# One level of Strassen's scheme for the two channel products of batches 2 to 7, on blocks of 288 positions

## The chip, the cores and the metric

The kernel runs on one core of one Trainium2 chip. The metric is the device time of one execution in microseconds; before the change it was 920.71 us (median of 3 runs, 919.43 to 924.66). The core's engines are called PE (matrix products), DVE, ACT and POOL (elementwise work, reductions, copies) and SP (which here only issues transfers). Each works its own instructions in program order, and they wait for one another by semaphores.

## What is computed

For each of 8 batches (8 heads, 576 positions, head size 64): a pooled attention (q, k, v averaged over 4 positions, the result repeated 4 times) plus a local attention (only positions less than 4 apart), then a mixer over 576 positions and 512 channels.

```
x = pooled_attention(q, k, v) + local_attention(q, k, v)    # [8, 576, 512]
h = max(x^T @ w_tok1, 0) @ w_tok2                           # 576 -> 256 -> 576, over positions
u = x + h^T
out = u + max(u @ w_ch1, 0) @ w_ch2                         # 512 -> 1536 -> 512, over channels
```

The last line holds the two channel products that the change is about.

## The kernel before, in words

Every value of a channel product is split into two f16 parts, hi and lo, and a product is three matmuls: hi x hi, hi x lo, lo x hi (`PASSES`, `mm3`, L116 to L118). Both weights, split and scaled, stay in SBUF for the whole run (`C1.fin`, `C2.fin`; tile names CW and CX). Channels lie on the partitions, positions along the free dimension, and a batch's 576 positions are worked as two chunks of 256 and 320 (`CHUNKS`).

For a chunk, `first` (L746) makes 12 blocks of 128 hidden channels, each of 4 x 3 matmuls into one of the three banks "m"; `first_up` (L760) takes each bank out twice: ACT writes relu as hi (L765), DVE the rest as lo (L767). `second` (L770) makes 4 blocks of 128 output channels, each of 12 x 3 matmuls; `second_up` (L784) has DVE scale the bank and add it to u (L793), and SP stores it (L794). So a batch has 2 x (12 x 12 + 4 x 36) = 576 matmuls of these.

Beside the products of batch b goes side work for the next batches, emitted in the same program order by a pacing rule: after each block `tick` (L898) takes as many side steps as a budget allows (`SIDE`, L888; a step counts by its written PE time). `side` (L735) is attention of batch b+1 in the order of the list `ORDER`, and then, by turns, its mixing (`mix`, L581) and the loads and poolings of batch b+2 (`ahead`, L723).

- `pooled` (L452), four times a batch: PE scores sd, DVE maximum and difference (pd), ACT exponential, PE transposes (td), ACT copy (ptd), PE product (ad), DVE normalization (rd, od; L494 to L496). The last one stores od into the rows of vw by transfers on ACT's queue (L502).
- `local` (L507), five tiles of 128 positions (the last 64): PE scores (sc), DVE mask, maximum, difference, ACT exponential, DVE sum and normalization (tile P), PE transposes (pT) and product with vw (av), ACT copies (pt, x).
- `mix`: x split for the position products (xh), two position products in banks t, u taken out of the banks (L661), its maximum over the whole chunk (L663, `everywhere` L565), and its split into the f16 parts uh (L680 ACT, L682 DVE).
- `load_v` (L401): POOL adds neighbouring rows of v (L425, L426). `load`, `load_w`: transfers of qk and vw on SP's queue.

PSUM has 8 banks: two pairs "gg", three "m", one "g". In batches 1 and later "g" serves the banks ad and pT of the attention and the small ones of `everywhere`.

Batch 0 and the preparation of the weights are ordered by a planner with costs and due times (`drive`, L157); from batch 1 on the loop at L890 writes the order.

Of the kernel before, what the change touches and what calls it, by code (L numbers as in the profile page):

```python
# [22 lines left out]
CHUNKS = ((0, 256), (256, 320))  # L23
TILES = ((0, 128), (128, 128), (256, 128), (384, 128), (512, 64))
OF_CHUNK = ((0, 1), (2, 3, 4))
NMAX = 320
PASSES = ((0, 0), (0, 1), (1, 0))
FR = 0.9
LIVE = 3
# [5 lines left out]
l0+l4 l0 l4 l2 l2 l4 l4 l1+l2 l1 l2 l3 l3 l4 l4 l3+l4 l3 l4"""  # L35
# [3 lines left out]
def tile_ups_attention_mixer(ctx, tc, qk, vw, vr, w1, w2, c1, c2, out):  # L39
# [12 lines left out]
    sb = ctx.enter_context(tc.tile_pool(name="sb", bufs=1))  # L52
    psum = ctx.enter_context(tc.tile_pool(name="psum", bufs=1, space=bass.MemoryType.PSUM))
    BUFS = dict(cw=6, h=5, w=4, xh=3, x=5, u0=4, u1=8, uh0=4, uh1=4, qk=4, qd=1, vw=2, vd=1, pt=2, od=1, sm=12, ev=8, sc=24)

    SLOTS = dict(gg=2, m=3, g=1, w=4)
# [9 lines left out]
    def T(shape, dt, tag, name):  # L66
        if tag == "w":
            return sb.tile(shape, dt, tag=slot(tag), name=name, bufs=1)
        return sb.tile(shape, dt, tag=tag, name=name, bufs=BUFS[tag])

# [16 lines left out]
    junk = sb.tile([128, 512], BF16, name="junk")  # L87
# [22 lines left out]
    PT = [sb.tile([128, H, 64], F32, name=f"P{i}") for i in range(3)]  # L110
# [4 lines left out]

    def mm3(ps, lhs, rhs, first, last, **kw):  # L116
        for i, (a, c) in enumerate(PASSES):
            nc.tensor.matmul(ps, lhs(a), rhs(c), start=first and i == 0, stop=last and i == 2, **kw)  # L118
# [111 lines left out]
    def token_weight(i, n, f):  # L230
        yield step("A", 0.0, ("W", "raw", i))
        raw = made["W", "raw"][i]
        if i < len(TILES):
            y = WY[i] = T([f.shape[0], n], F32, "u1", f"W1_y{i}")
# [18 lines left out]
    def singles(n, name):  # L253
        return [sb.tile([128, 512], F32, name=f"{name}{i}") for i in range(n)]
# [70 lines left out]
    class Second(Channel):  # L325
# [26 lines left out]
        def loads(self):  # L352

            self.raws = made["C2", "raw"] = []
            for i in range(NF):
# [3 lines left out]
                else:  # L359
                    if i % 2 == 0:  # L360
                        yield step("S", 0.1, *(("av", 0, t) for t in range(len(TILES))), *([("C2", "read", i - 4), ("C2", "read", i - 3)] if i >= 8 else []))
                        two = T([128, 2, 1024], U32, "vw", f"C2_raws{i}")
                    t = two[:, i % 2]
# [5 lines left out]
    C1.place = singles(NF + 2, "CW")  # L369
# [3 lines left out]
    short = TILES[-1][1]  # L373
    x_last = [sb.tile([128, 4, 2, D], F32, name=f"x_last{i}") for i in range(2)]
    for t in (W1[-1].bitcast(F32), *x_last):
        nc.gpsimd.memset(t[short:], 0.0)
    W2 = [sb.tile([128, 2, S], F32R, name=f"W2_{k}") for k in range(2)]
    W2_y = sb.tile([128, 2, S], F32, name="W2_y")
    WY = {len(TILES) + 2 * k + j: W2_y[:, k, HS * j:HS * j + HS] for k in range(2) for j in range(2)}
    W1_PIECES = [(u32(w1[s0:s0 + n]), 256) for s0, n in TILES]  # L380
# [20 lines left out]
    def load_v(st):  # L401
# [4 lines left out]
        def fetch(i):  # L406
            pr, g = divmod(i, 2)

            tag = "w" if st.b > 1 else "x" if st.b or i < BUFS["x"] else "xh"
# [4 lines left out]
        early = {0: 8, 1: 5}.get(st.b, 0)  # L414
# [15 lines left out]
    def load_w(st):  # L430
        st.vw = []
        for h in range(2):
            t = T([128, HG, 256], F32, "vw", f"vw{st.b}_{h}")
            for par in range(2):
                nc.sync.dma_start(t[64 * par:64 * par + 1 + WB].rearrange("p g c -> p (g c)"), vw[st.b, h, par])
            st.vw.append(t)
# [15 lines left out]
    def pooled(st, pr):  # L452
# [37 lines left out]
        if pr == 0:  # L490
            st.od = T([G, 2, 2, 4, D], F32, "od", f"od{b}")
        r = T([G, 2, 2], F32, "sm", f"rd{b}_{pr}")
# [3 lines left out]
        nc.vector.tensor_tensor(st.od[:, :, :, pr], ps[:, :, :, :D], r.unsqueeze(3).to_broadcast([G, 2, 2, D]),  # L496
                                ALU.mult)
        if pr == 3:
            yield step("A", 0.2, ("vw", b), at=e)
            for h in range(2):  # L500
                for par in range(2):
                    nc.scalar.dma_start(st.vw[h][64 * par + 1 + WB:64 * par + KB],  # L502
                                      st.od[:, h, par].rearrange("p a d -> p (a d)"))
# [3 lines left out]
    def local(st, t):  # L507

        b = st.b
        s0, n = TILES[t]  # L510
        nb = n // QB
# [3 lines left out]
        for hp in range(4):  # L515
            for j in range(nb):
                g = s0 // QB + j
# [5 lines left out]
        pp = PT[(len(TILES) * b + t) % 3]  # L523
# [27 lines left out]
        for hp in range(4):  # L551
            for j in range(nb):
                h, g = divmod(s0 // QB + j, HG)
                for par in range(2):
                    p = slice(64 * par, 64 * par + KB)
                    nc.tensor.matmul(ps[QB * j:QB * j + QB, par, D * hp:D * hp + D], pt[p, hp, QB * j:QB * j + QB],  # L556
                                     st.vw[h][p, g, D * hp:D * hp + D], start=True, stop=True)
        make(("av", b, t), e)
        e = yield step("A", 0.59, give="gg")
        x = st.x[t] = x_last[b % 2] if n == short else T([n, 4, 2, D], F32, "x", f"x{b}_{t}")  # L560
# [20 lines left out]
    def mix(st):  # L581
# [3 lines left out]
        st.hid, st.acc, banks, umx = [], [], {}, []  # L585
# [14 lines left out]
        def products():  # L600
            for t in range(NT):
# [4 lines left out]
                for f in range(2):  # L606
                    if b == 0:
                        n = TILES[t][1]
# [6 lines left out]
            for ch in range(2):  # L615
                s0, N = CHUNKS[ch]
                for c in range(4):
                    e = yield step("P", 1.2, *(("W", "split" if b else "y", NT + i) for i in range(4)), ("hid", b),
                                   *([("over", b - 1, 0)] if b and ch == 0 else []), take="" if c % 2 else f"gg>{b}")
                    if c % 2 == 0:  # L620
                        banks[ch, c // 2] = P2(f"t2_{b}_{ch}_{c}")
                    whole = banks[ch, c // 2][:, c % 2]
                    ps = whole[:, :N]
                    for i, t in enumerate(OF_CHUNK[ch]):
                        o = TILES[t][0] - s0
# [344 lines left out]
```

## Time and profile before

| | |
|---|---|
| Median of 3 runs | 920.71 us (919.43 to 924.66) |
| Profiled execution: time; span of the profile | 923.04 us; 921.2 us |
| Granted PE clock, mean | 0.992 |
| Product matmuls (L118, c) | 2 x 2304, 304.5 and 304.8 us busy |
| Product matmuls of batches 2, 3, 4, 5, 6, 7 begin at | 300.0, 409.9, 519.1, 628.6, 737.7, about 847 us |
| Transfers | 68.29 MB, mean 74 GB/s |

How to read it. Times are microseconds from the span's start unless marked ns. A group's line names the line of the code, the engine, the operation, output<-input, shapes and count; then its busy time, the mean of one in ns, and the engine's idle time just before with what ended it. Busy times by stretch give for each engine the time in which it had at least one instruction under way. Instructions may overlap their neighbours, so means times counts can exceed the time that a row of them takes. A chain piece is a stretch of the chain of work that ended last. The product matmuls of batch 0 begin at 82.4 us.

### The profile page before, as it was taken

How to read it: one execution, taken by the hardware profiler on the slowest of the kernel's cores; microseconds unless marked ns; L12 is line 12 of the kernel's file. 1: busy time of each engine (PE TensorE's matmuls, PEld its weight loads, DVE VectorE, ACT ScalarE, POOL GpSimd, SP SyncE). 2: the span in 40 equal slices, each digit the busy share in tenths (PEclk: the TensorE clock that was granted, in tenths of full speed). 3: DMA queues.
4: the chain of work that ended last, by engine and by line, in shares of the span. 5: the costliest groups of instructions: out<-in, count | busy, mean ns of one | idle time of the engine just before them, and what ended most of it. 6: DMA issues, size and time to landing. Idle time of an engine off the chain costs nothing.

```text
span 921.2 us, 25682 instructions
## 1 busy us (share of the span) xinstructions
PE 886.2 (96%) x11371; PEld 703.8 (76%) x11376; DVE 477.8 (52%) x1167; ACT 294.6 (32%) x622; POOL 108.3 (12%) x191
## 2 busy tenths in 40 slices
PE   8598999999999998999999999999999999999998
PEld 4466788889777886778867797787877788777876
DVE  8678895665532755247542565327553275324221
ACT  3368454232321414124131332314232141422120
POOL 7351400121200030000300003000130000000000
PEclk9799999999999999999999999999999999999999
DMA  8894503411700035000520006200170000000000
GB/s 238 232 314 159 160 9 94 138 49 38 219 2 23 9 106 151 9 22 3 183 73 8 23 14 198 47 15 17 37 213 8 23 9 26 14 8 22 13 12 29
DMA packets 28222, 68.29 MB, mean 74 GB/s; under 512 B 3504, under 2 KB 14000, under 8 KB 26864
## 3 DMA queue, kind: packets, MB, share of 16 engines
q1 hardware_dynamic: 25552, 64.30, 23.5%
q10 hardware_dynamic: 2560, 2.36, 0.9%
q8 instruction: 89, 1.46, 0.7%
q14 instruction: 21, 0.17, 0.1%
HBM read 54.85 MB, written 9.44 MB: 70 GB/s over the span
## 4 chain that ended last, share of the span: by engine, by line
PE 79%; DMA 9%; DVE 8%; issue 1%; ACT 1%; SPq 1%; POOL 0%; ACTq 0%; DVEq 0%; POOLq 0%
PE c L118 52%; PE t L118 10%; DMA qk<-in_qk_dram 4%; PE ad L488 3%; DMA vw<-od 3%; PE sc L520 2%; PE av L556 2%; PE t L626 2%; PE td L479 2%; DVE uh L682 1%; PE t L609 1%; PE pT L543 1%; DMA vr<-in_vr_dram 1%; PE sd L461 1%; PE t L630 1%
## 5 line engine op out<-in xcount | busy, mean ns | idle before, releaser
L118 PE MATMUL c<-h,CX 128*128 128x256 f16 (+1 forms) x2304 | 304.8, 286 | 0.0
L118 PE MATMUL c<-uh,CW 128*128 128x256 f16 (+1 forms) x2304 | 304.5, 286 | 0.4 <-DVE h L767 0.2
L118 PEld LDWEIGHTS <-CW 128*128 128x128 f16 x2304 | 218.8, 98 | 66.4 <-issue 12.5
L118 PEld LDWEIGHTS <-CX 128*128 128x128 f16 x2304 | 217.9, 98 | 58.4 <-issue 1.8
L767 DVE SCALAR_TENSOR_TENSOR h<-c,h 128x256 f16<-128x256 f32 (+1 forms) x192 | 87.2, 455 | 137.6 <-ACT h L765 137.0
L765 ACT ACTIVATE h<-c 128x256 f16<-128x256 f32 (+1 forms) x192 | 78.1, 407 | 186.8 <-PE c L118 186.8
L425 POOL TENSOR_TENSOR vr<-vr 72x256 f32<-72x256 f32 x64 | 46.6, 727 | 480.2 <-ACT ptd L482 263.6
L793 DVE SCALAR_TENSOR_TENSOR u<-c,io,u 128x256 f32<-128x256 f32 (+1 forms) x64 | 33.0, 515 | 106.4 <-PE c L118 105.1
L661 ACT COPY u<-t 128x256 f32<-128x256 f32 (+1 forms) x64 | 25.5, 398 | 136.8 <-PE t L118 106.1
L663 DVE TENSOR_REDUCE umx<-t 128x1 f32<-128x256 f32 (+1 forms) x64 | 29.3, 458 | 69.5 <-ACT u L661 53.8
L118 PE MATMUL t<-W,hid 128*128 128x256 f32 (+1 forms) x336 | 58.0, 308 | 0.0
L118 PE MATMUL t<-xh,W 128*128 128x512 f32 x210 | 57.3, 411 | 0.0
L561 ACT COPY x<-av 128x512 f32<-128x512 f32 x32 | 18.7, 585 | 101.3 <-PE av L556 101.2
L118 PEld LDWEIGHTS t<-W,hid 128*128 128x128 f32 x336 | 46.4, 189 | 0.0
L556 PE MATMUL av<-vw,pt 47*32 47x64 f32 x2304 | 34.9, 228 | 10.5 <-DMA vw<-od 6.3
L118 PEld LDWEIGHTS t<-xh,W 128*128 128x128 f32 x210 | 37.9, 188 | 8.0
L556 PEld LDWEIGHTS av<-vw,pt 47*32 47x32 f32 x2304 | 27.9, 107 | 19.8 <-issue 10.4
L488 PE MATMUL ad<-vd,ptd 72*72 72x65 f32 x512 | 38.6, 228 | 0.8 <-ACT ptd L482 0.8
L680 ACT ACTIVATE uh<-u,us 128x256 f16<-128x256 f32 (+1 forms) x64 | 29.5, 523 | 30.2 <-DVE us L124 28.6
L488 PEld LDWEIGHTS ad<-vd,ptd 72*72 72x72 f32 x512 | 37.2, 145 | 2.2 <-issue 0.8
L447 DVE TENSOR_REDUCE qd<-qk 128x72 f32<-128x288 f32 x64 | 25.9, 447 | 21.9 <-DMA qk<-in_qk_dram 21.9
L472 ACT ACTIVATE pd<-pd 72x576 f32<-72x576 f32 x32 | 21.9, 684 | 44.5 <-DVE pd L469 44.4
(114 smaller groups left out, 851.3 us busy)
## 6 DMA issues: line engine op xcount, KB each, us to landing
qk<-in_qk_dram SPq DMA_DIRECT2D x32, 579.0 KB
vw<-in_vw_dram SPq DMA_DIRECT2D x32, 351.0 KB
vr<-in_vr_dram SPq DMA_DIRECT2D x64, 144.0 KB
C_raw<-in_c_dram SPq DMA_DIRECT2D x16, 512.0 KB
out_dram<-u SPq DMA_DIRECT2D x32, 160.0 KB
C_raws<-in_c_dram SPq DMA_DIRECT2D x8, 512.0 KB
out_dram<-u SPq DMA_DIRECT2D x32, 128.0 KB
vw<-od ACTq DMA_DIRECT2D x32, 72.0 KB
```

Source lines behind the costliest of these rows:

```text
L118: nc.tensor.matmul(ps, lhs(a), rhs(c), start=first and i == 0, stop=last and i == 2, **kw)
L425: nc.gpsimd.tensor_add(t[:, 0:2], t[:, 0:2], t[:, 2:4])
L447: nc.vector.tensor_reduce(o, q[:, h], axis=AX.X, op=ALU.add)
L472: nc.scalar.activation(pd, pd, AF.Exp, scale=0.125 / 16)
L488: nc.tensor.matmul(ps[:, g, par], pt[:, par, kg, G * g:G * g + G], st.vd[:, kg, 2 * pr + par], start=kg == 0, stop=kg == 1)
L556: nc.tensor.matmul(ps[QB * j:QB * j + QB, par, D * hp:D * hp + D], pt[p, hp, QB * j:QB * j + QB], st.vw[h][p, g, D * hp:D * hp + D], start ...
L661: nc.scalar.copy(u, ps)
L663: nc.vector.tensor_reduce(umx[ch][:, c:c + 1], ps, axis=AX.X, op=ALU.max, apply_absolute_value=True)
L680: nc.scalar.activation(t[:, 0], st.u[ch][c], AF.Copy, scale=s)
L765: nc.scalar.activation(ht[:, 0], ps, AF.Relu)
L767: nc.vector.scalar_tensor_tensor(ht[:, 1], ps, 0.0, ht[:, 0], ALU.max, ALU.subtract)
L793: nc.vector.scalar_tensor_tensor(us[c], banks[c], io, us[c], ALU.mult, ALU.add)
```

## The change

Batches 0 and 1 keep their products, with both chunks 288 wide. For batches 2 to 7 the inputs are cut in 2 x 2 blocks (B11 to B22: two halves of the channels, two halves of 288 positions), the weights likewise, and seven block products take the place of eight (Winograd's form of the scheme). Sums of the weights' blocks are made once, beside batch 1's products, half on DVE and ACT and half on POOL, split into f16 parts, and stored to device memory together with the plain blocks. From batch 2 on they are streamed from there through a ring of six buffers on SP's queue, 26 units a batch (six of 524 KB, six of 393 KB, fourteen of 393 KB). Sums of the inputs' blocks are made per batch from u.

```diff
+HALF = 288
+TILES = ((0, 1, 2, 3), (4, 5, 6, 7), (9, 10, 11, 12), (13, 14, 15, 16), (8, 17))
+SIDE = 72.0
+WEIGHT = dict(P=1.0, V=0.5, A=0.25)
...
+    HOME = dict(cw="B", h="B", SG="B", SV="B", h7="B", f="B", uh0="A", uh1="A", wy="A", ring="A", uh="A", f2="A")
-    SLOTS = dict(gg=2, m=3, g=1, w=4)
+    SLOTS = dict(gg=2, m=3, g=1, w=3)
...
-                    nc.scalar.dma_start(st.vw[h][64 * par + 1 + WB:64 * par + KB],
+                (nc.scalar if b < 2 else nc.sync).dma_start(
+                    st.vw[64 * par + 1 + WB:64 * par + KB].rearrange("p g h c -> p g (h c)"),
```

The input's blocks and their sums, in `mix`, after the previous batch's first product:

```diff
+        def combined():
+            yield step("V", 0.0, ("u", b), ("first", b - 1))
+            big = yield from everywhere(f"um{b}", umx[0])
...
+            def split(name):
...
+                    nc.scalar.activation(hi, x, AF.Copy, scale=s)
+                    nc.vector.scalar_tensor_tensor(lo, x, s, hi, ALU.mult, ALU.subtract)
...
+            split("B11")
+            less("B12", "B11", "T1")
+            split("T1")
+            less("B22", "T1", "T2")
+            split("T2")
+            split("B22")
+            split("B21")
+            less("B22", "B12", "T3")
+            split("T3")
+            less("B21", "T2", "T4", block["T2"])
+            split("T4")
```

The weights' sums (`weight_sums`), one step after each block of products of batch 1; `eng` is DVE for odd p and POOL for even p, `put` splits a sum (hi by ACT or POOL, lo by `eng`) and `keep` stores it:

```diff
+        for C in (C1, C2):
+            for p, f in enumerate(FIRSTS):
...
+                after_products(eng.tensor_tensor(t, a21, a22, add))
+                eng.tensor_tensor(t[:, 0], t[:, 0], t[:, 1], add)
+                put("S1", t[:, 0])
+                keep("A11", a11)
+                yield
```

(and likewise S2, S4, S3, A12, A22). The first product: for each n of six pairs of hidden blocks, products in the order B11, T3 (of pair n-1), T1, T2, T4 (of n-1), B22, B21. `product` is six matmuls. Bank X takes B11, then T2, T3 and T4 are added to it; bank Y takes T1, then B22; B21 goes to the bank "g". Between the additions, copies are taken out. `late(k, ...)` puts work k products later; `over` emits it and takes side steps.

```diff
+                product(p.X, p.a[:, 0], "B11", True)
+                p.s = F("s", n)
+                nc.scalar.copy(p.s, p.X)
+                over()
...
+                product(q.X, q.b[:, 1], "T3", False)
+                nc.vector.tensor_add(q.y, q.X, q.y)
+                def after22(q=q, n=n):
+                    lo_relu(q.h, "B22", q.y)
+                    positive(q.u, q.y, ALU.subtract, q.u)
+                    q.t2 = F("t2", n - 1)
+                    positive(q.t2, q.y, ALU.add, q.t1)
+                late(1, lambda q=q: hi(q.h, "B22", q.y))
+                late(2, after22)
+                late(3, lambda q=q: (hi(q.h, "T2", q.t2, AF.Copy), hi(q.h, "T3", q.u, AF.Copy)))
+                late(4, lambda q=q: (lo(nc.gpsimd, q.h, "T2", q.t2), lo(nc.gpsimd, q.h, "T3", q.u)))
...
+                product(p.Y, p.a[:, 1], "T1", True)
+                nc.scalar.copy(p.y, p.Y)
...
+                product(p.X, p.a[:, 2], "T2", False)
+                nc.scalar.copy(p.u, p.X)
...
+                product(q.X, q.b[:, 2], "T4", False)
+                hi(q.h, "B21", q.X)
+                positive(q.t4, q.X, ALU.subtract, q.t2)
+                late(1, lambda q=q: (lo_relu(q.h, "B21", q.X), hi(q.h, "T4", q.t4, AF.Copy)))
+                late(3, lambda q=q: lo(nc.gpsimd, q.h, "T4", q.t4))
...
+                product(p.Y, p.a[:, 3], "B22", False)
+                nc.vector.tensor_add(p.u, p.Y, p.u)
+                late(1, lambda p=p: nc.scalar.activation(p.u, p.u, AF.Relu))
...
+                z = P1(f"cz{b}_{n}")[:, :HALF]
+                product(z, p.b[:, 0], "B21", True)
+                nc.vector.tensor_add(p.s, z, p.s)
```

After it come hi and lo of B11 and T1 (`after11`, `last1`). The second product: for each of two output halves o, seven products of 18 matmuls, and after each DVE adds the bank to u:

```diff
+            for n in SECOND:
+                w = fetched_units.pop(0)
...
+                product(at[kind], w, of[n], new)
+                nc.vector.scalar_tensor_tensor(u, at[kind], io, u, ALU.mult, ALU.add)
+                fetch()
+                if n == "A22":
+                    nc.sync.dma_start(out[b, 128 * o + 256:128 * o + 384], high)
+                elif n == "A12":
+                    nc.sync.dma_start(out[b, 128 * o:128 * o + 128], low)
+                tick(PRODUCT)
```

Around it: the weights' memory is given free in two pools, A (first weights, then ring, uh and f2) during batch 1 and B (second weights, then h7 and f) after it; the rows of positions are regrouped in tiles so that each half has two full ones and a part of the last; `WEIGHT` makes DVE and ACT steps count in the pace; the tiles w go from four buffers to three, x from five to four, P from three to two (from batch 2 on), and vw is one tile of the same size.

More of the change, by code (lines that the diff above doesn't have):

```diff
@@ L114, in tile_ups_attention_mixer @@
         nc.vector.tensor_copy(p[:, :, 1 + WB:KB], rep.unsqueeze(1).to_broadcast([128, H, QB // 4]))
+    last_product = [None]
     def mm3(ps, lhs, rhs, first, last, **kw):
         for i, (a, c) in enumerate(PASSES):
[L118 removed]
+            last_product[0] = nc.tensor.matmul(ps, lhs(a), rhs(c), start=first and i == 0, stop=last and i == 2, **kw)
     def pow2(src, f, inv, s, least=2.0 ** -60):
@@ L359, in loads @@
                 else:
[L360 to L363, printed above, removed]
+                    yield step("S", 0.1, *(("av", 0, t) for t in range(len(TILES))), *([("C2", "read", i - 4)] if i >= 8 else []))
+                    if i == 4:
+                        four = T([128, 4, 1024], U32, "vw", "C2_raws")
+                    t = four[:, i % 4]
                 in_turn(nc.sync.dma_start(t, u32(c2[i])))
@@ new lines, in second_blocks, with product @@
+    def second_blocks(st, tick):
+        b, H = st.b, st.H
+        io = T([128, 1], F32, "sc", f"io{b}")
+        nc.vector.tensor_mul(io, st.ui[0], ic)
+        PRODUCT = 18 * HALF * 0.425e-3
+        of = dict(A11="B11", A12="B21", S4="B22", A22="T4", S1="T1", S2="T2", S3="T3")
+        def product(ps, w, x, first_):
+            i = PARTS.index(x)
+            for k in range(6):
+                for j, (a, c) in enumerate(PASSES):
+                    nc.tensor.matmul(ps, w[:, k, a], H[k][:, i, c], start=first_ and k == j == 0,
+                                     stop=k == 5 and j == 2, skip_group_check=True)
+        for o in range(2):
+            low, high = st.u[o], st.u[o + 2]
+            into = dict(A11=low[:, 0], A12=low[:, 0], S2=low[:, 1], S4=low[:, 1], S1=high[:, 1], S3=high[:, 1], A22=high[:, 0])
+            at = {}
+            for n in SECOND:
+                w = fetched_units.pop(0)
+                kind = {"S1": "Y", "S4": "Y", "A12": "Z"}.get(n, "X")
+                new = kind not in at
+                if new:
+                    at[kind] = P1(f"dz{b}_{o}")[:, :HALF] if kind == "Z" else bank(o if kind == "X" else 2, f"d{kind}{b}_{o}")
+                product(at[kind], w, of[n], new)
+                u = into[n]
+                nc.vector.scalar_tensor_tensor(u, at[kind], io, u, ALU.mult, ALU.add)
+                fetch()
+                if n == "A22":
+                    nc.sync.dma_start(out[b, 128 * o + 256:128 * o + 384], high)
+                elif n == "A12":
+                    nc.sync.dma_start(out[b, 128 * o:128 * o + 128], low)
+                tick(PRODUCT)
+            make(("over", b, o), now[0])
@@ L911, in tile_ups_attention_mixer @@
                 u.go()
-                tick(CHUNKS[ch][1])
+                tick(HALF, 24 * S)
+                next(sums, None)
+            if ch:
+                open_pool("A", "stream", "right")
+                make(("first", b), now[0])
+                for _ in range(BUFS["ring"]):
+                    fetch()
             g, u = Run(second(st, ch, banks)), Run(second_up(st, ch, banks))
@@ L918, in tile_ups_attention_mixer @@
                         u.go()
-                    tick(CHUNKS[ch][1])
+                    tick(HALF, 24 * S)
+                    next(sums, None)
+        assert next(sums, None) is None
+        open_pool("B", "hidden", "left")
     while work.next is not None:
         work.go()
+    for g in opened.values():
+        g.__exit__(None, None, None)
 _INS = ["qk", "vw", "vr", "w1", "w2", "c1", "c2"]
```

341 lines of the change are left out of this document (271 added, 70 removed).

## Prediction

> **What bounds the kernel now.** I read the profile's first part, then busy times by stretch (one middle batch, batch 0 beside the end of its set-up, the last batch), the chain of waits, the groups, and the order of time in a dense spot.
>
> ```profile
> PE 886.2 (96%) x11371; PEld 703.8 (76%) x11376; DVE 477.8 (52%) x1167; ACT 294.6 (32%) x622; POOL 108.3 (12%) x191
> ```
> ```profile
> core 0: us, PE busy (x) PEld busy (x) DVE busy (x) ACT busy (x) POOL busy (x), PEclk, DMA share, GB/s
> 82.00:197.00 115.00, 113.86 (x1473) 92.08 (x1474) 86.04 (x207) 48.67 (x97) 21.10 (x35) 1.00 0.31 88
> ...
> 519.10:628.60 109.50, 106.98 (x1408) 86.46 (x1407) 53.69 (x135) 32.79 (x71) 9.46 (x17) 1.00 0.22 61
> ...
> 846.35:917.85 71.50, 71.48 (x582) 56.79 (x582) 17.50 (x41) 11.64 (x28) 0.00 (x0) 1.00 0.05 17
> ```
> ```profile
> PE 79%; DMA 9%; DVE 8%; issue 1%; ACT 1%; SPq 1%; POOL 0%; ACTq 0%; DVEq 0%; POOLq 0%
> ...
> 846.35 71.50 PE c L118 x582
> ```
>
> TensorE is the bound, at full clock: batch 4 (519.1 to 628.6) takes 109.5 us, and PE idles for 2.5 of them, while DVE is at 49% and ACT at 30%. Batch 7 has no side work and is products without a gap: 71.50/582 = 0.123 us a matmul, 0.123 x 576 = 70.8 us a batch. So a middle batch is 70.8 of products, 36.2 of side work on PE, 2.5 idle.
>
> **What is removed.** Of a batch's 576 product matmuls (mean 288 columns) stay 6 x 7 x 6 = 252 in the first and 2 x 7 x 18 = 252 in the second product, all of 288 columns: 72 fewer. Over six batches 432 x 0.123 = 53.1 us. It is all on the path, since PE is; what is left to ask is what comes to stand beside it.
>
> **What takes its place on the vector engines.**
>
> ```profile
> L767 DVE SCALAR_TENSOR_TENSOR h<-c,h 128x256 f16<-128x256 f32 (+1 forms) x192 | 87.2, 455 | 137.6 <-ACT h L765 137.0
> L765 ACT ACTIVATE h<-c 128x256 f16<-128x256 f32 (+1 forms) x192 | 78.1, 407 | 186.8 <-PE c L118 186.8
> L425 POOL TENSOR_TENSOR vr<-vr 72x256 f32<-72x256 f32 x64 | 46.6, 727 | 480.2 <-ACT ptd L482 263.6
> L793 DVE SCALAR_TENSOR_TENSOR u<-c,io,u 128x256 f32<-128x256 f32 (+1 forms) x64 | 33.0, 515 | 106.4 <-PE c L118 105.1
> ```
> ```profile
> L682 DVE SCALAR_TENSOR_TENSOR uh<-u,us,uh 128x320 f16<-128x320 f32 x32 | 16.4, 564 | 0.6 <-ACT uh L680 0.6
> ...
> L682 DVE SCALAR_TENSOR_TENSOR uh<-u,us,uh 128x256 f16<-128x256 f32 x32 | 14.7, 496 | 4.5 <-ACT uh L680 4.4
> ...
> L597 DVE TENSOR_TENSOR xh<-x,xh 128x512 fp32r<-128x512 f32 x28 | 19.1, 685 | 11.6 <-ACT xh L595 11.6
> ```
>
> First product: each of six pairs had 4 DVE and 4 ACT operations (L767, L765); it gets 11 DVE, 11 ACT and 3 POOL. DVE: 66 x 0.455 = 30.0 us instead of 10.9. ACT: 66 x 0.407 = 26.9 instead of 9.8. POOL: 18 at 0.727 x 288/256 = 0.82, 14.7 us, an estimate.
> Second product: 14 x 0.515 = 7.2 us of DVE instead of 4.1.
> Splitting the input (L682 before): three blocks of two 288 halves (6 x 0.53) and four whole ones of 576 (0.53 + 288 x (0.564 - 0.496)/64 = 0.84 each) make 6.5, eight subtractions at 0.455 make 3.6: 10.1 us of DVE instead of 8 x 0.53 = 4.2.
>
> Which stage gets them decides. A pacing rule hands out side work: 72 units over 0.9 x 62 us of product time. Attention's steps come to about 39 units by their written costs, so they end after about 30 us of products: attention lies beside the first product (31.0 us), mixing beside the second. These rows are stretches of 409.5 to 519.1 us for single tiles: the local probabilities P, the pooled maxima mxd, the pooled sums rd, then the mixing banks t.
>
> ```profile
> 409.50:519.10 109.60, 2.89 (x20) 2.15 (x20) 11.64 (x25) 2.29 (x5) 1.00 0.21 61
> ```
> ```profile
> 409.50:519.10 109.60, 6.25 (x12) 1.00 0.21 61
> ```
> ```profile
> 409.50:519.10 109.60, 3.01 (x12) 1.00 0.21 61
> ```
> ```profile
> 409.50:519.10 109.60, 18.19 (x98) 14.43 (x98) 5.05 (x10) 4.38 (x10) 1.00 0.21 61
> ```
>
> Attention takes 11.6 + 6.3 + 3.0 = 20.9 us of DVE a batch. Of PE's 36.2 the mixing takes 18.2, so attention 18.0. The first product's stage needs of PE 31.0 + 18.0 = 49.0, of DVE by durations 30.0 + 20.9 = 50.9. But durations of neighbours overlap:
>
> ```profile
> 437.73 0.47 DVE L531 TENSOR_REDUCE mx<-P 128x8 f32<-128x304 f32 x1
> 438.12 0.47 DVE L527 TENSOR_TENSOR P<-sc,mask 128x304 f32<-128x304 f32 x1
> 438.50 0.47 DVE L532 TENSOR_TENSOR P<-P,mx 128x304 f32<-128x304 f32 x1
> 438.88 0.47 DVE L531 TENSOR_REDUCE mx<-P 128x8 f32<-128x304 f32 x1
> 439.38 0.47 DVE L532 TENSOR_TENSOR P<-P,mx 128x304 f32<-128x304 f32 x1
> ```
>
> Operations of 0.47 start 0.38 us apart where one doesn't need the one ahead, 0.50 where it does (438.88 to 439.38). The new ones mostly don't: 66 x 0.38 + 20.9 = 46.0 us. DVE comes to 94% of PE's 49.0, just under the bound. [...]
>
> So PE should stay the bound, with stalls. The added waits: T2 waits for ACT's copy of the bank that it adds to, T4 for DVE's sum out of it, each with two products (1.5 us) between; what queues behind on PE is side work too. The block B21 uses bank g, which attention shares: nine evacuations a batch, 0.75 us each by rd (3.01/4), against six such products. The pooled result's store into vw goes from ACT's queue to SP's, behind the streamed units, and PE's av products wait for it:
>
> ```profile
> vw<-od ACTq DMA_DIRECT2D x32, 72.0 KB
> ```
> ```profile
> PE av L556 <- DMA vw<-od: 6.3, 5, 2.5
> ```
>
> I price a middle batch's stage at +4.0 us: two hits of bank g (1.5), the later store (1.0), late copies and sums (1.5). Ends: 0, since between 82 and 197 us DVE was at 75% and PE idled only 1.1 us; and 50.9 + 4.0 - 49.0 = +5.9, if no durations overlap. I take 4.0, as 94% is above that row's 75%. Five batches (2 to 6): +20. Batch 7 has no side work: DVE 25.1 against PE 31.0; +1.2 for the two-product waits, between 0 and +5.
> The second stage needs of DVE 7.2 + 10.1 + 13.6 (mixing and pooling: 53.7 - 20.9 - 10.9 - 4.1 - 4.2) beside 31.0 + 18.2 us of PE: covered. If not, the next batch starts late by up to the 10.1.
>
> **Batch 1 pays for the weights' blocks.** Twelve groups of sums, half on DVE: two of 512 elements (0.685) and ten of 256 (at 0.455, a little high) are 5.9 us, six groups 35.5, plus 24 ACT copies that DVE waits for; on POOL 18 x 0.727 x 6 = 79 us by the same count. DVE goes from 53.7 to 89 of about 109 us, 82%, nearest the 75% row, in bursts, on the queue that frees the product banks: +5 (0 to +14). At its end h7 and f lie where the old weights were: the first copy of batch 2 waits for the last sums and stores: +3 (0 to 8).
>
> **The stream.** 6 x (524 + 393) + 14 x 393 KB = 11.0 MB a batch: 178 GB/s in batch 7 (62 us), and with the 61 GB/s of before about 175 in the others.
>
> ```profile
> GB/s 238 232 314 159 160 9 94 138 49 38 219 2 23 9 106 151 9 22 3 183 73 8 23 14 198 47 15 17 37 213 8 23 9 26 14 8 22 13 12 29
> ```
>
> A slice reached 314, and six units ahead are some 15 us of products, so it is hidden: 0. Behind qk loads or a wait of SP it lags, within these 15 us. Uncovered, at the 160 of slice 5, it costs 11.0/0.160 - 62 = 7 us a batch.
> The tail's last store has 295 KB for 160: +0.3. Even halves, regrouped tiles, three w and two P buffers: 0 each, behind products; uncovered they are in the +4.0.
>
> **Sum.** 923.0 (profiled execution) - 53.1 + 20 + 1.2 + 5 + 3 + 0.3 = 899.4. The profiled one is 2.3 above the median 920.7: **897 us**.
>
> **Rivals.**
> 1. All hidden: DVE's 46.0 fits under 49.0 and the planner's order already keeps steps apart. 923.0 - 53.1 + 0.3 - 2.3 = 868. Against it: ACT too has 26.9 plus attention's share in that stage, and each of the three engines waits in order for the others.
> 2. The gain is swallowed: the DVE durations don't overlap (each new operation waits for PE or ACT). +5.9 x 5, +5 in batch 7, +14 in batch 1, +3.3: 919.4.
> 3. Slower, POOL locks DVE out. These two lie side by side:
>
> ```profile
> 450.73 1.01 DVE L532 TENSOR_TENSOR P<-P,mx 64x304 f32<-64x304 f32 x1
> ```
> ```profile
> 442.75 0.72 POOL L425 TENSOR_TENSOR vr<-vr 72x256 f32<-72x256 f32 x1 [88.02 <-ACT ptd L482]
> ...
> 450.68 0.72 POOL L425 TENSOR_TENSOR vr<-vr 72x256 f32<-72x256 f32 x1
> ```
>
> The same operation took 0.47 at 438.50, when POOL had been idle for long; started 0.05 us into a POOL operation, 1.01. If each of the 18 new POOL operations (0.82) holds one of the new DVE operations for its length, the stage needs 46.0 + 14.7 = 60.7 of DVE against 49.0, +11.7, more than the 8.9 saved; batch 7 25.1 + 14.7 - 31.0 = +8.8; batch 1 +14: 923.0 - 53.1 + 58.5 + 8.8 + 14 + 3.3 - 2.3 = 952. It decides for slower from about four in five of these operations hitting. Against it: POOL works only some 30% of the stage, and only two-input SBUF operations were stretched; the PSUM ones, 30 of 66, have no such row. [...]
> 4. The stream is late: +7 x 6: 939.
> That fewer matmuls are issued is sure by count; that they take 0.123 us each is not in doubt, as 256 and 320 columns average 288.
>
> **How the numbers follow.** Forecast (880 to 913) 0.48; all hidden (866 to 880) 0.20; swallowed (913 to 926) 0.16; POOL lock (926 to 952) 0.13; stream late 0.03. Under 0.5% (4.6 us) a measurement of this kernel can't tell from no change: faster below 916.1, slower above 925.3. Of "swallowed" 0.05 falls to faster, 0.10 to same, 0.01 to slower: faster 0.73, same 0.10, slower 0.17. The range 866 to 924 leaves out some 0.17 above and next to nothing below.
>
> **What would show it.** Right: 504 product matmuls a batch, middle batches of about 105 us with PE idle 6 to 7, batch 7 near 63; DVE 75 to 85 busy a batch. Wrong: PE idle before T4 or B21 released by DVE, DVE operations near 1 us beside POOL ones (rival 3), PE waiting for unit loads (4), batch 1 over 117 us.

## The result, and the profile after

The changed kernel takes 959.95 us (median of 4 runs, 955.95 to 961.94) against 922.68 (919.43 to 925.16): a ratio of 1.0401 [1.0347, 1.0454]. It is slower by 4%, where 897 us, 2.6% below the 920.71 of the first runs, was forecast. The forecast's range ended at 924, so sign and range are wrong.

First part and clock row of the page after:

```profile
PE 879.6 (92%) x11017; PEld 686.2 (71%) x11021; DVE 654.4 (68%) x1527; ACT 397.5 (41%) x886; POOL 264.6 (28%) x394
...
PEclk9689999898999979899999999799997999999999
```

The matmuls are gone from the count (11371 to 11017), but PE was busy for only 6.6 us less, and eight of the clock row's forty digits are below nine, where before only one was. Busy time by stretch, one row a batch (set-up, then batches 0 to 7; the last row holds the end of the program too):

```profile
core 0: us, PE busy (x) PEld busy (x) DVE busy (x) ACT busy (x) POOL busy (x), PEclk, DMA share, GB/s
0.00:87.90 87.90, 71.41 (x953) 45.88 (x958) 61.82 (x149) 41.90 (x84) 37.41 (x70) 0.86 0.84 262
87.90:206.70 118.80, 113.10 (x1444) 91.84 (x1444) 83.22 (x198) 46.86 (x95) 17.70 (x30) 0.97 0.42 112
206.70:329.10 122.40, 112.20 (x1414) 89.64 (x1413) 90.32 (x187) 38.70 (x86) 80.89 (x116) 0.96 0.39 119
329.10:451.30 122.20, 107.77 (x1343) 83.89 (x1341) 85.26 (x197) 50.17 (x114) 28.18 (x39) 0.92 0.51 148
451.30:561.90 110.60, 102.93 (x1343) 81.40 (x1341) 75.97 (x182) 48.25 (x110) 24.10 (x35) 0.97 0.53 159
561.90:673.50 111.60, 103.75 (x1344) 81.82 (x1343) 76.39 (x182) 48.38 (x110) 23.84 (x35) 0.95 0.53 159
673.50:785.80 112.30, 103.94 (x1344) 81.94 (x1342) 76.22 (x182) 48.67 (x110) 24.56 (x35) 0.95 0.53 158
785.80:894.10 108.30, 102.82 (x1352) 81.42 (x1350) 71.60 (x175) 49.95 (x113) 13.72 (x18) 0.98 0.39 119
894.10:960.20 66.10, 61.66 (x498) 48.39 (x495) 33.57 (x81) 24.63 (x65) 14.20 (x18) 1.00 0.49 159
```

The same cut through the trace of before gives 82.4, 110.8, 106.8, 109.9, 109.2, 109.4, 109.2, 109.4 and 74.1 us, at a clock of 1.00 from batch 0 to batch 6. So, in us:

| stretch | set-up | b0 | b1 | b2 | b3 | b4 | b5 | b6 | b7 and end |
|---|---|---|---|---|---|---|---|---|---|
| measured | +5.5 | +8.0 | +15.6 | +12.3 | +1.4 | +2.2 | +3.1 | -1.1 | -8.0 |
| by the forecast | 0 | 0 | +5 | -1.9 | -4.9 | -4.9 | -4.9 | -4.9 | -7.4 |

Set-up to batch 2 lose 41 us, most of them where not one product was taken away; batch 7 gains as forecast; the middle batches miss by 4 to 8 each. What PE waited for (engine, line, waited for; us in all, times, longest):

```profile
PE av L572 <- DMA vw<-od: 13.4, 7, 3.1
PE cx L982 <- DVE y L1028: 11.7, 7, 3.6
...
PE ad L503 <- ACT ptd L497: 5.5, 2, 5.2
...
PE cy L982 <- DVE u L873: 4.6, 1, 4.6
PE ad L503 <- DVE od L512: 3.8, 2, 3.1
```

Before, `av` waited for the store of od 6.3 us. One such place, in batch 4, in order of time:

```profile
608.95 0.90 PE L982 MATMUL cx<-uh_T,wb 128*128 128x288 f16 x6 [2.22 <-DVE y L1028]
609.78 0.42 PE L572 MATMUL av<-vw,pt 47*32 47x64 f32 x2
611.73 1.17 PE L572 MATMUL av<-vw,pt 47*32 47x64 f32 x62 [1.53 <-DMA vw<-od]
613.57 0.63 PE L572 MATMUL av<-vw,pt 47*32 47x64 f32 x18 [0.68 <-ACT x L577]
614.13 1.62 PE L982 MATMUL cz<-uh_B,wb 128*128 128x288 f16 x6
```

PE stands still for 2.22 and 1.53 us. The granted clock is 1.00 up to 609 us and 0.50 from 610 to 620, so it fell right behind the first gap, and for 10 us PE ran at half speed: six product matmuls take 1.62 us where six took 0.90. So PE lost time here twice. The store itself, in the chain of waits:

```profile
602.67 9.01 DMA vw<-od
```

The order in which PE's instructions are laid out shows why this wait is new. From the last `ad` to the block of 62 `av` matmuls, a middle batch had 72 product matmuls before (8.9 us at 0.123); now it has 46 (5.7 us), because the new pace packs attention denser, and the store takes 9. (One pair of `av` goes ahead of the block, before the change after 47.)

### The profile page after: what moved, and what is told of

The parts are those of the page before. It is cut to its first block, busy times and chain, and to the rows that moved or that the text cites. A ratio compares the mean times of both kernels' runs of the same rounds, so it can differ in the third digit from the quotient of the medians.

```text
span 960.2 us, 26341 instructions
## 1 busy us (share of the span) xinstructions
PE 879.6 (92%) x11017; PEld 686.2 (71%) x11021; DVE 654.4 (68%) x1527; ACT 397.5 (41%) x886; POOL 264.6 (28%) x394
## 3 DMA queue, kind: packets, MB, share of 16 engines
q1 hardware_dynamic: 70576, 143.16, 49.6%
## 5 line engine op out<-in xcount | busy, mean ns | idle before, releaser
L982 PEld LDWEIGHTS <-wa 128*128 128x128 f16 x864 | 84.6, 99 | 33.7 <-issue 7.3
L1104 PEld LDWEIGHTS <-wc_S 128*128 128x128 f16 x864 | 81.7, 98 | 24.8 <-issue 4.4
L982 PEld LDWEIGHTS <-wb 128*128 128x128 f16 x648 | 61.8, 100 | 32.5 <-issue 15.1
L982 PE MATMUL cx<-uh_T,wb 128*128 128x288 f16 x432 | 69.1, 287 | 11.7 <-DVE y L1028 11.7
L135 PE MATMUL c<-uh,CW 128*128 128x288 f16 x576 | 77.0, 290 | 0.0
L135 PE MATMUL c<-h,CX 128*128 128x288 f16 x576 | 76.2, 288 | 0.0
L1104 PEld LDWEIGHTS <-wc_A 128*128 128x128 f16 x648 | 62.1, 98 | 18.5 <-issue 2.7
L135 PEld LDWEIGHTS <-CW 128*128 128x128 f16 x576 | 55.6, 99 | 16.0 <-issue 1.9
L135 PEld LDWEIGHTS <-CX 128*128 128x128 f16 x576 | 55.2, 99 | 14.8 <-issue 0.5
L572 PE MATMUL av<-vw,pt 47*32 47x64 f32 x2304 | 40.0, 264 | 23.3 <-DMA vw<-od 13.4
L135 PE MATMUL t<-W,hid 128*128 128x288 f32 x336 | 59.0, 309 | 1.0 <-DVE hid L668 0.8
```

The costliest lines, as they stand in the source:

```text
L135: last_product[0] = nc.tensor.matmul(ps, lhs(a), rhs(c), start=first and i == 0, stop=last and i == 2, **kw)
L982: nc.tensor.matmul(ps, w[:, a, 128 * k:128 * k + 128], uh[x][:, k, c], start=first_ and k == j == 0, stop=k == 1 and j == 2, skip_group_ch ...
L1104: nc.tensor.matmul(ps, w[:, k, a], H[k][:, i, c], start=first_ and k == j == 0, stop=k == 5 and j == 2, skip_group_check=True)
```

## The experiments

**Theory A**: the store lands too late for `av`, and the gap halves PE's clock behind it. **Rivals**: DVE, by the loads it waits for or by POOL (rival 3 on record); the stream; the weights' sums; the pace itself.

### What it is not

`held_pool`: the pooling of the next batch's q and k on DVE waits (from batch 3 on) for the first t1 matmul, so that no DVE work queues behind a late qk load.

```diff
-            nc.vector.tensor_reduce(o, q[:, h], axis=AX.X, op=ALU.add)
+            after_mixing(st, nc.vector.tensor_reduce(o, q[:, h], axis=AX.X, op=ALU.add))
```

> Edit: from batch 3 on DVE's pooling of q and k for the next batch waits for the first position product of this batch, so it no longer stands in DVE's queue in front of the sum y that TensorE's T4 waits for. Theory A (the lost time is TensorE waiting for late transfers, through DVE and at av, plus the half clock that follows): the wait of cx for y (3.6, 2.2, 2.7 us in batches 3 to 5) is gone, part of the half-clock time after it too, middle batches 3 to 6 us shorter: about 945 us. Theory B (DVE is overloaded or locked out by POOL in the first product's stage): DVE has the same work, so the stage keeps its 62 us and the time stays at 958 to 962.

957.16 us, 1.0374 [1.0343, 1.0404]. PE's waits for y fell from 11.7 to 0.2 us, but the wait of `av` for the store grew to 20.9: a second lateness stood behind the first one. Where 945 was expected, the time is next to the 958 to 962 of a cause elsewhere, so the loads alone aren't it.

`od_act`: the store goes back to ACT's queue in all batches (`nc.scalar.dma_start`).

> Edit: the pooled result's stores into vw go on ACT's queue in all batches, as before the change, the streamed units stay on SP's. Theory A: if the queue that issues them is what delays av, the wait of av for the store (1.5 to 3.5 us a batch) goes and the time falls by 5 to 15 us; if the store is slow because its data stands behind qk and the units on the same transfer engines, nothing changes (within 3 us). Theory B: no change.

1021.33 us, 1.1069 [1.1006, 1.1132], the largest miss of the study. PE waited 49.6 us for DVE's h, up to 13.1 at once, and `av` still 20.0 us for the store. ACT around one such place, in order of time:

```profile
511.80 1.43 ACTq L517 DMA_DIRECT2D vw<-od  x2
513.27 0.41 ACT L1001 ACTIVATE h<-cx 128x288 f16<-128x288 f32 x1 [1.38 <-DMA vw<-od]
...
532.25 0.44 ACT L1001 ACTIVATE h<-t 128x288 f16<-128x288 f32 x1 [17.82 <-DVE t L1012]
```

ACT's queue took the two stores in 1.43 us, and three more operations of ACT ran right behind them; the 17.82 us are a wait for DVE's t. This t stood on DVE behind the poolings of the next batch's q and k for four heads, and they waited for loads of qk. DVE's wait for these loads in the whole kernel, which was 13.4 us in 6 places in the changed kernel:

```profile
DVE qd L462 <- DMA qk<-in_qk_dram: 44.4, 18, 7.0
```

So the edit moved more than the store: DVE's poolings and its t came to stand in another order (why was not followed up), and at this place the loss is that of late loads in front of PE's work, not of the store's issue. What the queue of the store is worth by itself, this run doesn't tell.

`no_stream`: six units are loaded once and used over and over (wrong weights from then on).

> Edit: six buffers are loaded once and used again for all units of batches 2 to 7; the 11 MB a batch aren't streamed (so the weights used are not the right ones). Theory A with the stream as the cause of the late transfers: qk and the store land in 2 to 4 us instead of 6 to 9, the waits of DVE for qk and of av for the store go, and with them the half clock: middle batches near 104 us, 920 to 930 in all. Theory B: no change in the first stage, 955 to 962.

962.80 us, 1.0435 [1.0405, 1.0465]: no gain. The traffic of batch 4 fell by half in its first stage (158 to 81 GB/s), and `av` waited for the store as long as before (13.1 us). The stream was rightly priced at 0; in `gap_split2` and `gap_nosums` below, without the merged store, PE waits for units 1.3 us at most.

`pool_memset`: POOL's `eng.tensor_tensor(h[:, i, 1], x, h[:, i, 0], ALU.subtract)` becomes `eng.memset(h[:, i, 1], 0.0)`.

> The changed kernel with the low halves that GpSimd makes in the first stages of batches 2 to 7 set to zero (so a part of the second product is left out): GpSimd reads nothing from the SBUF there. Rival 3 of the prediction (GpSimd's two-input operations hold VectorE's back): the first stages fall to 50 to 56 us and the time to 900 to 930. Theory A: VectorE's two-input operations already take 455 to 531 ns as forecast, so the time stays within 8 us of 960.

955.15 us, 1.0337 [1.0295, 1.0379], within the 8 us that theory A allowed, and the first stages of batches 3 to 6 stayed where they were (65.3, 64.2, 64.8 and 58.7 us; 63.6, 64.5, 65.3 and 59.7 in the changed kernel). Rival 3 is out for the middle batches.

`old_pace`: `SIDE = 42.0`, `WEIGHT = dict(P=1.0)` as before the change.

> The pacing of before (42 units, VectorE's and ScalarE's steps not weighed) with the rest of the change. Theory A: between the last ad and the first av stand 48 products instead of 46, so the wait for the store stays near 3 us a batch with its half clock, but the sums and the remaining steps are spread otherwise: 945 to 975. If the pacing itself were the cause (rival D: denser steps in front, empty PE behind) the time would fall to 900 to 925.

970.37 us, 1.0505 [1.0457, 1.0553]: the new pace is better than the old one here.

### The scheme, or the edits around it?

`old_products`: batches 2 to 7 take the old eight products, all other edits stay.

```diff
-        return [splits(), products(), takes(), scaled() if b < 2 else combined()]
+        return [splits(), products(), takes(), scaled()]
```

> All edits of the change but the scheme itself: batches 2 to 7 take the eight products of the old scheme on halves of 288 positions, with no sums, no stream. By the theory that the loss is in the pacing and the store (A), the first stages keep the wait of av and its half clock: with 63 more us of matmuls in the six batches than the changed kernel has, less what they hide, the time is 960 to 1000. By a rival (C: the scheme's own sums on VectorE and ScalarE are what hold the matmuls up), the other edits cost nothing and the time is that of before, 920 to 930, with batches of 109 us.

952.34 us, 1.0315 [1.0272, 1.0359]: the edits that I had priced at 0, or at 1.0 a batch for the later store, cost 28 us without any Strassen in the kernel. `av` waits for 21.5 us in all ("issue" 17.2, the store 4.3).

`no_store`: base `held_pool`; no store of od from batch 2 on.

> The store od to vw is left out in batches 2 to 7 (the pooled rows of vw are loaded from device memory ahead instead, so the pooled part of the attention is another). Theory A: PE has nothing to wait for between ad and av, the half-clock periods of the middle batches go, the first stages fall from 60 to 65 to 50 to 56 us, the time to 905 to 930. Theory B: stages stay above 60 us, the time within 10 us of 960.

949.69 us, 1.0267 [1.0230, 1.0305], where theory A had expected 905 to 930. The first stages of batches 3 to 6 fell to 56.6 to 59.7 us and the batches to 104.1 to 106.6 (108 to 112 in `held_pool`), but batch 1 grew to 145. One wait there, of `ad` for ptd, is 11.8 us long; the rest was not followed up, so the total says little.

`gap`: `held_pool`, a step of 8 units without work between the last `ad` and the first `av` from batch 3 on, and `SIDE = 80.0`.

```diff
+            if st.b > 2 and nexts["p3"] is None and not parted:
+                parted.append(1)
+                yield step("P", 8.0)
```

> Theory A (after the last matmul of ad, the middle batches issue 46 product matmuls, about 46 x 0.123 = 5.7 us, before the first av, while the store od to vw takes 8 to 9 us to land; the gap that follows and the half clock behind it cost 12 to 15 us a batch): with about 71 to 100 products between ad and av in batches 3 to 7 (8.7 to 12 us) the wait of av for the store falls from about 3 us to under 1 us, no half-clock period lies in the first stage, and the first stages of batches 3 to 6 fall from 60 to 65 us to 50 to 56; the time falls by 30 to 45 us against 960, to 915 to 930. [...]

944.94 us, 1.0222 [1.0184, 1.0260], above the 915 to 930 expected. Batches 3 to 6 went from 111.4, 110.8, 112.2 and 108.3 us (`held_pool`) to 106.2, 108.5, 106.4 and 107.1; batch 1, which got the denser pace but no gap, rose to 134.9 and ate half of it.

`filler`: `held_pool` with eight idle matmuls (mean 431 ns) after the last `ad`.

```diff
+            for i in range(8):
+                op = nc.tensor.matmul(ps[:, 0], W2[0][:, 0, :128], W2[0][:, 0, :512], start=True, stop=True)
```

> Next batch's q and k pooled after the first t1 matmul (as in held_pool), and in batches 2 to 7 eight idle matmuls (128x512, written into av's bank and overwritten by av) four products after the last ad, so that PE issues 2 to 3 us of work for nothing where it would wait for the store. The idle matmuls take as long as the wait that they replace, so any gain is the clock's: by theory A the half-clock periods in the first stages go and the time falls from 957 to 925 to 940. If the half clock costs little (rival), the time stays at 952 to 965.

956.90 us, 1.0344 [1.0301, 1.0387]: no gain. The first stages of batches 3 to 6 went from 64.2, 63.3, 65.0 and 59.8 us (`held_pool`) to 62.3, 64.2, 60.7 and 60.1. Only batch 5 gained much: its clock rose from 0.92 to 1.00. In batch 4 the clock stayed low (0.92; 0.95 in `held_pool`). Eight fillers keep PE busy for 2.3 us a batch (13.9 us for all 48), more than the stages fell on the mean. So bridging the gap didn't keep the clock reliably here (mean of the whole run 0.964, against 0.959); the next runs take a cause of the gap away.

### The store by halves

The change had merged od's four stores of 72 KB into two of 144, since vw became one tile with both halves interleaved. Tiles 0 and 1 read only the first half, but wait for both stores whole. `split_store` lays vw out half by half again, and loads it so (the part for the store is shown):

```diff
-            for par in range(2):
-                (nc.scalar if b < 2 else nc.sync).dma_start(
-                    st.vw[64 * par + 1 + WB:64 * par + KB].rearrange("p g h c -> p g (h c)"),
-                    st.od[:, par].rearrange("p h a d -> p (h a d)"))
+            for h in range(2):
+                for par in range(2):
+                    (nc.scalar if b < 2 else nc.sync).dma_start(
+                        st.vw[64 * par + 1 + WB:64 * par + KB, h], st.od[:, par, h].rearrange("p a d -> p (a d)"))
```

> The changed kernel with vw half by half and od stored by four transfers of 72 KB, first half first. Theory A (the store lands 3 us late, and the gap halves PE's clock for 3 to 10 us): the first half lands 4 to 5 us after od instead of 8 to 9, the first stages of batches 3 to 6 fall from 60 to 65 us to 52 to 57, and the time from 960 to 920 to 935, the rest of the loss staying in batches 1 and 2 (the weights' sums). Rival: four transfers queue behind the same loads and units, the last of them lands as late as now, and the time stays within 8 us of 960.

940.15 us, 1.0168 [1.0133, 1.0204]: 2.3% of the time of before, 21 us, from this alone, though the time is above the 920 to 935 expected, and the first stages of batches 3 to 6 are 58.0 to 62.5 us for 52 to 57 expected. PE's wait for the store fell from 13.4 us in 7 places to 2.0 in one. In batch 4 the block of `av` now begins 8.5 us after the end of od, without a wait for the store. Set-up and batch 0 gain 8 us, batch 2 gains 6.5, batch 1 loses 3.2, and batches 3 to 6 gain 2.4 each on the mean. One gap of 2.50 us, for DVE's y, stands alone in batch 4 here, and a granted clock of 0.50 from 599 to 605 us follows it: groups of six matmuls at 599.8 and 603.2 took 1.62 and 1.65 us, 0.90 ahead of the gap.

The kernel before, in its batch 4, shows what the halves were good for:

```profile
565.05 0.84 PE L556 MATMUL av<-vw,pt 47*32 47x64 f32 x62
...
572.08 0.81 PE L556 MATMUL av<-vw,pt 47*32 47x64 f32 x58 [0.89 <-DMA vw<-od]
```

There od ended at 556.65 and the last of the store landed at 572.03, 15.4 us later, which is later than in the changed kernel (10.1). But the first block began after 8.4 us without a wait; only further on had `av` to wait, for 0.89 us.

`old_split` does the same to `old_products`:

> The eight old products on the new halves and tiles, but vw laid out half by half again and od stored by four transfers of 72 KB, those of the first half first, as before the change. If the merged store (two transfers of 144 KB, which the first tile's av waits for although it uses one half) makes the 28 us that the edits beside the scheme cost, the waits of av for the store (21 us in all, 'issue' and store together) fall to under 5, and the time to 922 to 932. If the regrouped tiles, the extra transposes and the pacing cost them, the time stays at 945 to 955.

931.27 us, 1.0055 [1.0025, 1.0086]: 24 us. The waits of `av` fell from 21.5 to 11.8 us, and the mean clock rose from 0.974 to 0.988. The merged store is the largest single cause found, with either scheme.

### The weights' sums

`gap_split2`: `split_store` and `gap` together, the gap from batch 2 on, batch 1 at the pace of 72.

> As best1 but with the sums shared six and six as in the change. If GpSimd's queue (v's pooling of batch 2 stands behind the sums) makes batch 1 long, six sums instead of eight take batch 1 from 136 us to 120 to 127 and the time to 925 to 933. If the sums' place is of no matter, 936 to 944 as best1.

930.94 us, 1.0067 [1.0034, 1.0100], within the 925 to 933 expected, though batch 1, at 129.7, is above its 120 to 127. `gap_nosums` leaves the sums out and stores the plain blocks:

> gap_split2 with the sums left out (the blocks themselves are stored as units, so the products of batches 2 to 7 are others); stores and stream stay. If the sums' work is what batches 1 and 2 lose: batch 1 at 108 to 113 us, batch 2 at 106 to 110, the time 895 to 910. If the stores on SyncE's queue or the stream cause it: batch 1 stays above 116, the time 918 to 930.

912.95 us, 0.9873 [0.9836, 0.9910], just above the 895 to 910 expected: 1.9%, 18 us, less than `gap_split2` takes. Batches 1 to 3 with the sums, then without:

```profile
198.60:328.30 129.70, 115.53 (x1417) 90.42 (x1414) 89.57 (x191) 37.69 (x84) 82.47 (x119) 0.94 0.38 119
328.30:439.10 110.80, 103.12 (x1340) 80.67 (x1340) 81.24 (x190) 50.61 (x117) 23.72 (x35) 0.98 0.52 155
439.10:544.00 104.90, 100.02 (x1344) 79.86 (x1342) 75.39 (x183) 47.91 (x110) 23.86 (x35) 1.00 0.54 169
```
```profile
205.40:312.60 107.20, 107.20 (x1417) 87.00 (x1415) 50.87 (x121) 29.03 (x60) 14.19 (x25) 1.00 0.32 93
312.60:420.80 108.20, 102.08 (x1340) 79.79 (x1340) 80.19 (x188) 51.30 (x117) 23.82 (x35) 1.00 0.51 153
420.80:526.60 105.80, 100.17 (x1344) 79.84 (x1343) 76.30 (x182) 47.81 (x110) 23.87 (x35) 1.00 0.56 167
```

These 18 us aren't the sums' work alone. Without the sums the stores of the blocks have no sums to wait for: all 126 of them run in batch 0, which takes 119.9 us there (113.9 in `gap_split2`), with 159 GB/s of traffic instead of 117, and none is left in batch 1. With the sums they run in batch 1 and into batch 2. So what batch 1 loses is due to the sums and their stores together, and no run parts the two.

Batch 1 without the sums is PE without a gap; with them PE idles 14.2 us and runs at 0.94. Its longest waits there, with the sums:

```profile
PE ad L508 <- ACT ptd L502: 5.0, 1, 5.0
PE ad L508 <- DVE od L517: 3.2, 1, 3.2
PE c L135 <- DVE h L857: 3.0, 1, 3.0
```

In the order of time the first is a wait of ACT for POOL's rows of v (6.7 us), which stood behind sums on POOL; in the second, od stood behind sums on DVE, one of them 1.94 us long. The third is of another kind: DVE had waited 4.5 us for a load of qk that was issued right behind two stores of sums on SP's queue, and h stood behind that. An operation of DVE with two inputs in SBUF also took longer in this batch, as rival 3 has it, with POOL busy for 82.47 us instead of 14.19: the same operation in batch 1 with the sums (797 ns), then without (519 ns).

```profile
L553 DVE TENSOR_TENSOR P<-P,mx 128x304 f32<-128x304 f32 x4 | 3.2, 797 | 0.1
```
```profile
L553 DVE TENSOR_TENSOR P<-P,mx 128x304 f32<-128x304 f32 x4 | 2.1, 519 | 0.1
```

That is 1.1 us for these four, and 3.9 us over all such operations that both runs have in batch 1. It is small beside the 22.5 us by which batch 1 is longer; how much of it reached PE was not measured. The sums' own operations (SV_sum, 128x256 f32) took from 416 to 746 ns, as the means of their lines.

`no_sums` had taken the sums out of the changed kernel itself:

> Edit: the weights' sums are left out; plain blocks are stored in their place (so the results of batches 2 to 7 are not the reference's). The prediction priced the sums at 5 and the batch boundary at 3; batch 1 is 15.7 us longer than before, with two waits of ad for ACT and DVE (5.2 and 3.1) and a half clock. If the sums are the cause, batch 1 falls from 122.5 to 107 to 110 and batch 2 from 122.2 by some 5: 938 to 945. If it is the stores or the order of batch 1 itself, batch 1 stays above 118.

959.41 us, 1.0398 [1.0292, 1.0504]: nothing gained. Batches 1 and 2 were 5 and 10 us shorter, batches 0 and 3 some 5 longer each. As long as the merged store stood, one gap gave way to the next.

Three runs moved the sums. In all three my edit moved the tag that picks ACT's copies and the buffers, but left the adds where the number of the group put them (even on POOL, odd on DVE). `best1` so changed only who rounds (ACT in four groups instead of six); in `early` half of batch 0's groups ran on DVE, in `late` two of its four.

> Three remedies together: od's store by halves, 8 us of products held between the last ad and the first av (batches 2 to 7), and of the twelve weight sums only four on VectorE and ScalarE (GpSimd takes eight instead of six), with the pacing of 80 units after batch 1. Theory A: middle batches at 104 to 107 us, batch 1 at 112 to 120, batch 2 at 108 to 114, batch 7 at 62: 905 to 925 us. Rival: GpSimd, about 11 us a sum, gets its eight sums done late and holds up the start of batch 2: 930 to 945.

941.01 us, 1.0186 [1.0147, 1.0225]; batches 1 and 2 took 135.8 and 117.6 us, batches 3 to 6 104.9 to 107.4. It doesn't tell what POOL's share costs.

> gap_split2 with the six sums of the first product's weights made by GpSimd in batch 0 and the six of the second product's shared by GpSimd and VectorE in batch 1. If crowding in batch 1 is the cause: batch 0 within 4 us of 113, batch 1 at 110 to 117, batch 2 at 106 to 112, the time 900 to 918. If the stores in batch 0 block SyncE's loads for batch 1 the gain is lost there: batch 0 above 120, the time over 930.

936.60 us, 1.0129 [1.0092, 1.0166]: batch 2 fell to 107.1 us, but batch 0 rose to 134.0 and batch 1 was 121.0.

> gap_split2 with every weight sum behind the next batch's pooled attention: four of the first product's on GpSimd in batch 0 after its last ad step, the other eight in batch 1 after batch 2's last ad step, four on GpSimd and four on VectorE. If the sums cost time because they stand ahead of v's pooling, of the copies of ptd and of od on GpSimd, ScalarE and VectorE, batch 0 stays within 4 us of 114, batch 1 falls from 130 to 108 to 114, batch 2 to 106 to 110, and the time to 908 to 920, faster than the kernel before. If their amount costs it, the loss moves to the end of batch 1 and to the start of batch 2: 925 to 935.

935.62 us, 1.0140 [1.0115, 1.0166]: batches 0 and 1 took 123.0 and 121.0 us. The loss moves with the sums.

`from3` leaves batch 2 to the old products, uses the new scheme from batch 3 on, and so has two batches for the twelve groups:

```diff
-        return [splits(), products(), takes(), scaled() if b < 2 else combined()]
+        return [splits(), products(), takes(), scaled() if b < 3 else combined()]
...
-                next(sums, None)
+                slots[0] += 1
+                if slots[0] % 2:
+                    next(sums, None)
```

> gap_split2 with batch 2 left to the old eight products, the new scheme in batches 3 to 7 alone, and the twelve weight sums spread over batches 1 and 2 instead of batch 1. If crowding is the cause: batch 1 at 108 to 115 us (130 in gap_split2), batch 2 at 109 to 116, batches 3 to 6 at 105.5 each, batch 7 at 62, the time 905 to 918, faster than the kernel before. If each sum costs its share wherever it stands, batches 1 and 2 together stay above 240 and the time at 925 to 938.

918.51 us (12 runs) against 923.53 (17): 0.9948 [0.9928, 0.9969], the version that beats both kernels, by half a per cent, and just outside the 905 to 918 expected. Batches 1 and 2:

```profile
199.60:315.30 115.70, 109.69 (x1415) 88.63 (x1414) 64.84 (x157) 34.16 (x76) 45.00 (x71) 0.97 0.29 87
315.30:428.90 113.60, 110.42 (x1499) 89.24 (x1498) 73.84 (x176) 36.70 (x80) 43.48 (x65) 1.00 0.38 112
```

229.3 us together against 240.5 in `gap_split2`, though batch 2 has 72 matmuls more. With DVE at 56 and 65% instead of 69 and 73, half of the loss is gone. So crowding is a good part; the rest, 12.6 us above the 216.7 of before, is not settled further.

## Why the prediction was wrong

- **The store, "the later store (1.0)": the step that failed most.** The vw tile with both halves in one had no term at all. I priced the move of the issue to SP's queue and read "vw<-od ACTq DMA_DIRECT2D x32, 72.0 KB" without setting it against the two stores of 144 KB in the diff. What counted is the latest byte that the first `av` waits for: its waits were 13.4 us with two stores of 144 KB, 2.0 with four of 72. Measured: 21 us in the changed kernel (8 of them ahead of batch 1, some 2.4 a middle batch), 24 with the old products, not five times 1.0.
- **"Late copies and sums (1.5)" hid another lateness.** A sign on record, PE idle before T4 for DVE, came: it is the 11.7 us for y. But its cause was poolings on DVE that waited for loads of qk (13.4 us). `held_pool` took it away, and the time hardly changed.
- **"+5 (0 to +14)" for batch 1 and "+3" for its end: the mechanism was right in part, the size too small.** The count was fair (POOL 82.47 us with the sums and 14.19 without, so 68 for 79 forecast; DVE 89.57 for 89). But I took PE's stalls from a row with DVE at 75%; the sums come in blocks that v, `ptd` and od stand behind, and their stores stand ahead of loads on SP's queue, which the sum left out. The sign on record came, batch 1 took 122.4 us. Measured: 18 us with their stores.
- **The clock had no term at all.** The sum priced a stall at its length. Mean clock fell from 0.992 to 0.952, and the kernel with it: in batches 3 to 5 PE idles 7.7 to 8.4 us, not much more than the 6 to 7 forecast, but is busy for 103 to 104 us. In `gap_split2` batch 3, at a clock of 1.00, is busy for 100.0. So some 3 to 4 us a middle batch go with the slow clock. Not every stall has this price: that batch idles for 4.9 us at full clock.
- **The order on PE.** "Attention ends after about 30 us of products" was right, and I asked only whether DVE could keep up. The same density took the products away from between od's store and `av`: 46 matmuls where 72 had stood. `gap` put 103 there, and with its denser pace took 1.5% off `held_pool`.
- **"Regrouped tiles" at 0** is short of a small sure term. The two parts of the last tile are now transposed apart. Groups of the whole kernel, before and after:

```profile
L626 PE MATMUL t<-ident,x_last 128*128 128x128 f32 x32 | 8.7, 273 | 0.0
```
```profile
L644 PE MATMUL t<-ident,x_last 128*128 128x32 f32 x128 | 19.6, 235 | 0.0
```

  10.9 us of PE over eight batches.
- **Right:** the removed matmuls; the stream at 0; the second stage's cover (47.0 us a middle batch for 49.2 of PE work forecast); batch 7 (-8.0 against -7.4); and the stage's +4.0, once store and order were mended: middle batches of 104.9, 105.7, 108.9 and 105.5 us in `gap_split2` for 104.6 forecast, with PE idle some 5 us in the first two. The stream's rate was added up wrongly (178 GB/s over 62 us is 11.0 MB; over 104.6 us and with the 61 of before it makes 166, not 175, and 158 to 159 were measured), without weight for the time.
- **Luck.** Rival 3 had the sign and nearly the size (952), by a mechanism that `pool_memset` rules out where I had put it, in the middle batches.

By ratios, in the order in which things were taken back: 1.0401, less 0.0233 for the store's halves, 0.0101 for gap, pace and held pooling, 0.0194 for the sums with their stores gives 0.9873, 913 us. The shares hang on this order: taken back first, the sums gave nothing (`no_sums`). The forecast without its 8 us for the sums is 889, so that some 20 us are left to 0.9873. The transposes' 10.9 and the 9 by which batch 0 is longer than before, with the blocks' stores in it, come to about that; that these are the whole of it is not shown.

## What to carry to other kernels

When a layout edit merges transfers, ask for each consumer which bytes it needs first and when the last byte of its transfer lands; a merged transfer can make the first reader wait for the whole (here 13.4 us of waits, 2.0 with the halves apart). When work is packed denser or taken off a bound engine, look at what had stood between each producer and its consumer: the removed work was also the cover of some latency (here 8.9 us of products became 5.7, beside a store of 9). One-time work needs a stage with slack on each queue that it joins, the queue of its stores too, judged by its longest block and not by the mean load (here 18 us for the sums with their stores, with DVE at 69% of batch 1 and one operation of a sum 1.94 us long).

## What was not expected of the hardware

One gap of 2.22 us in batch 4 of the changed kernel, after 6 us in which PE never stood still, was followed by a granted clock of 0.50 for some 10 us: groups of six matmuls went from 0.90 to 1.62 us. In `split_store` a gap of 2.50 us was followed by 0.50 for some 6 us: 1.62 and 1.65 us for six matmuls.
